# A spectral mixer with a feed-forward layer: the last inverse DFT in three matmuls of 128 rows for four pairs, in place of four of 96

## The chip, the cores and the metric

The kernel runs on one core of a Trainium2 chip. The metric is the device time of one execution in microseconds, the median of several runs; less is better. The matmul engine TensorE (PE in the profile; PEld is its loading of the stationary operand), VectorE (DVE), ScalarE (ACT) and GpSimd (POOL) run their own instruction streams in order; SyncE (SP) issues the DMAs, also in order.

## The reference

The input `x` is 8 × 3008 × 256. Along the 3008 time steps a real DFT is taken, the spectrum goes through a complex linear layer with a bias and a soft threshold, and comes back by the inverse DFT; the result goes through a feed-forward layer.

```python
X = np.fft.rfft(x, axis=1)
Yr = Xr @ w_r - Xi @ w_i + b_r
Yi = Xr @ w_i + Xi @ w_r + b_i
Yr = np.sign(Yr) * np.maximum(np.abs(Yr) - 0.01, 0)      # Yi likewise
y = np.fft.irfft(Yr + 1j * Yi, n=3008, axis=1)
h = y @ w_in                                              # 256 -> 2048
out = (h - np.tanh(h)) @ w_out                            # 2048 -> 256
```

## The kernel before

**The DFT in two steps.** 3008 = 64 × 47. The first step (`Forward`, and `Stacked` for batches 3 to 7) is a DFT over 47 and gives 24 frequencies; the second (`Spectrum.transform`, line 332) one over 64, 128 columns a matmul, the table read from another start for each frequency. After the linear layer `inverse` (lines 410 to 412) undoes the step over 64 and `put` writes the result `zo` to DRAM as `z`: 32 pairs of 96 rows (2 parities × real and imaginary × 24 frequencies) by 256 features.

**The last step**, which the change touches, is `Unit`: for a pair, 96 rows of `z` go to 94 time steps (2 × 47). A `Unit` takes up to four pairs. Its `load` (lines 484 to 495) brings the table (96 × 94 for each pair, into a piece of the tile `shared`) and `z` (tile `zin`); the features are the stationary operand in two halves of 128 columns, the table is the moving one. So for each pair and each half there is a matmul with 96 rows and 94 columns (line 504), in plain fp32, which the profile records as two MATMULs each. `both(k)` (line 522) does two pairs for both halves into one PSUM bank, 2 × 188 columns, and ScalarE copies these 376 columns into `raw`, or into `spill` for columns that belong to the next chunk (line 556). In the first stage `time(t)` does one half of all pairs of a unit.

**Chunks.** The feed-forward layer works on the 8 · 3008 columns in 47 chunks of 512 (`Chunk`). 94 does not divide 512, so the units of a chunk are cut so that a pair belongs to the chunk in which it begins: 4 pairs and then 1 or 2, and fewer at the end of a batch. The columns that stick out go to `spill`, at most 92 of them, and GpSimd copies them back (`unspill`, line 568) when `raw` is free. `sums` and `operands` make the operands of the feed-forward layer from `raw` on GpSimd and ScalarE. From chunk 3 on, this layer saves one matmul in eight in its first product (`Pair`, line 671); line 600 is the second product. Both stand on TensorE with 256 and 512 columns.

**The order of the work.** All engines and the DMA queue are recorded in an order written by hand. The feed-forward layer runs as a row of slots, 16 to a chunk, of some 3 us each; `plan` puts every other step into a slot with a rank: loads 0, the first transform's split 0.5 and its matmuls 7, `Spectrum.dft` 6, `inverse` 2.5, `Unit` 8, `sums` 9. In `run` (line 764) an inverse moves behind the `dft` of its slot if the slot has no step of rank 3, 4, 7 or 8. `unit_slots` looks for slots for the units in a window before the chunk is wanted, slots with a `dft` alone first and then the calmest; a unit's load is put five slots ahead of its first matmul, but not before the last `z` of its batch is written (`done_at`). Two `zin` buffers and two pieces of `shared` take turns. Within a slot, the steps share two PSUM buffers for all that is not the feed-forward layer.

Two places are tight, where a batch's first chunk is due soon after its last spectrum: chunk 5 (batch 1 begins in it; its unit has slot 74 and its load slot 72, the last `inverse` slot 71) and chunk 11 (batch 2; last `inverse` in slot 164, load in slot 165, matmuls in slot 168). In slots 71 to 86 the first transform of batch 2 runs, whose loads of x (eight, tile `xt`, two buffers, line 215) are put five slots ahead of their first matmul.

Of the kernel before, what the change touches and what calls it, by code (L numbers as in the profile page):

```python
# [18 lines left out]
LAM = 0.01  # L19

# [12 lines left out]
def dft_constants():  # L33
# [30 lines left out]
    i2 = i2.reshape(96, NP * 94)  # L64
# [4 lines left out]
def spectral_ffn(ctx, tc, x, w_r, w_i, b_r, b_i, w_in, w_out, x_twice, f1, f1s, f2, i1, i2, out):  # L69
    nc = tc.nc  # L70
    P = 128
# [179 lines left out]
    class Stacked:  # L251
# [3 lines left out]
        def load(self):  # L255
            if self.p == 0:
                a_dram[self.b] = dram.tile([2, NP, 96, D], F32, name=f"a_{self.b}", tag="a")
            if self.p % 6 == 4:
                self.xt = shared_piece("x2", 2 * 4 * 94 + 4 * D, 4 * D, 1).rearrange("p (a d) -> p a d", a=2)
# [45 lines left out]
    class Spectrum:  # L305
# [6 lines left out]
        def load(self):  # L312
# [4 lines left out]
            if self.b > 2:  # L317
                self.al = shared_piece("al", 2 * 4 * 94, 2 * D, 2)
                nc.sync.dma_start(out=self.al, in_=rows(a_dram[self.b][1], self.jp))
# [161 lines left out]
    class Unit:  # L481
        def __init__(self, b, p, n, home=None):
            self.b, self.p, self.n, self.home = b, p, n, home

        def load(self):
            if self.home is None:
# [4 lines left out]
                nc.sync.dma_start(out=self.table, in_=i2[:, self.p * 94:(self.p + self.n) * 94])  # L491
            else:
                self.zt = piece(self.home, [96, 4, D], F32, "zin")
                self.table = i2t[:, self.p * 94:(self.p + self.n) * 94]
            nc.sync.dma_start(out=self.zt[:, :self.n, :], in_=z_dram[self.b][self.p:self.p + self.n].rearrange("a p d -> p a d"))

        def time(self, t):
            ps = bank("ps_i2")
            self.multiply(ps, t)
            self.take(ps, t)  # L500

        def multiply(self, ps, t, at=0, which=None):
            for j, k in enumerate(which or range(self.n)):
                nc.tensor.matmul(  # L504
                    ps[:, at + j * 94:at + (j + 1) * 94], self.zt[:, k, t * P:(t + 1) * P],
                    self.table[:, k * 94:(k + 1) * 94], start=True, stop=True,
                )

        def pieces(self, k=0, n=None):
            first = self.b * S + (self.p + k) * 94  # L510
            lo, hi = first, first + (n or self.n) * 94
            while lo < hi:
                c = next(c for c in range(NCH) if begin[c] <= lo < begin[c] + sizes[c])
                end = min(hi, begin[c] + sizes[c])
                yield chunks[c], lo - begin[c], slice(lo - first, end - first)
                lo = end

        def take(self, ps, t):
            for chunk, at, cols in self.pieces():
                chunk.take(t, at, ps[:, cols])  # L520

        def both(self, k):
            ps = bank("ps_i2")
            m = min(2, self.n - k)
            n = m * 94
            for t in range(2):
                self.multiply(ps, t, t * n, range(k, k + m))
            pv = ps[:, :2 * n].rearrange("p (t n) -> p t n", t=2)
            for chunk, at, cols in self.pieces(k, m):
                chunk.take_both(at, pv[:, :, cols])  # L530
# [3 lines left out]
    class Chunk:  # L534
# [12 lines left out]
        def take(self, t, at, src):  # L547
# [4 lines left out]
            else:  # L552
                nc.scalar.copy(out=self.home(at, n)[:, t], in_=src)

        def take_both(self, at, src):
            nc.scalar.copy(out=self.home(at, src.shape[2]), in_=src)

        def home(self, at, n):
            if at > 0 or n >= 94:
                return raw[:, :, at:at + n]  # L560
            if self.spill is None:
                self.spill = work.tile([P, 2, 96], F32, name="spill", tag="spill")
                self.spilled = n
            return self.spill[:, :, :n]
# [284 lines left out]
    def plan():  # L849
# [22 lines left out]
        for b in range(2, B):  # L872
# [17 lines left out]
        for c in range(FIRST + 1, NCH):  # L890
            lo, hi = (-(-CT * k // 94) for k in (c, c + 1))
            units = []
            while lo < hi:
                n = min(4, hi - lo, NP - lo % NP)
                units.append(Unit(lo // NP, lo % NP, n))
                lo += n
            late = [u for u in units if c == first_chunk[u.b]]
            early = [u for u in units if c != first_chunk[u.b]]
            for some_units, window in ((early, (-14, -9 if late else -6)), (late, (-10, -6))):
                at = unit_slots(c, sum((u.n + 1) // 2 for u in some_units), window, max([done_at.get(u.b, 0) + 2 for u in some_units], default=0))  # L900
                for u in some_units:
                    mine = [at.pop(0) for _ in range(0, u.n, 2)]
# [57 lines left out]
    with tc.manual_schedule(engines={E.PE, E.Activation, E.DVE, E.Pool, E.SP}):  # L960
# [39 lines left out]
        i2t = work.tile([96, NP * 94], F32, name="i2", tag="i2", bufs=1)  # L1000
# [49 lines left out]
        for i in range(NU + 1):  # L1050
# [29 lines left out]
            if i in (5, 8):  # L1080
                sl = slice(0, 10 * 94) if i == 5 else slice(10 * 94, None)
# [10 lines left out]
        early_units = [Unit(0, 4 * k, 4, k) for k in range(5)] + [Unit(0, 20, 2, 5)]  # L1092
# [172 lines left out]
```

## Time and profile before

| | |
|---|---|
| median of 3 runs | 2609.38 us (2609.1 to 2612.08) |
| profiled execution | 2607.96 us |
| its span, first to last instruction | 2606.2 us |
| mean granted TensorE clock | 0.996 |
| from HBM, to HBM | 136.56 MB, 90.70 MB |
| loads of `z` for the last step | 93, of which 46 of 384 KB |

A row of a group reads: line, engine, operation, output<-inputs, shapes and count, then after the bar the busy time in us and the mean ns of one, then the idle time of the engine ahead of it and what ended it. A row of the timeline reads: start and length in us, engine, line, operation, and in brackets the idle time ahead of it with what ended that. Rows of SPq are DMA issues; in the list of DMA issues the last number is the median us from issue to landing. A row of the waits reads: who waited, for whom, us in total, times, longest.

### The profile page before, as it was taken

The page shows a single profiled execution, that of the slowest core. Times are in us where ns is not written, and L with a number is a line of the kernel's source. Part 1 is how long each engine was busy: PE and PEld are TensorE (multiplying, and loading weights), DVE is VectorE, ACT ScalarE, POOL GpSimd, SP SyncE. Part 2 cuts the span into 40 slices and gives each one's busy share as a digit, 9 for nine tenths or more (in the row PEclk, how much of TensorE's full clock was granted, in tenths as well). Part 3 has the DMA queues.
Part 4 walks back from the last instruction along what each step waited for, and adds up shares of the span by engine and source line. Part 5 has one row for each costly group of instructions (what it writes and reads, how often), then busy time and mean ns, then how long its engine had stood idle before and what let it go on. Part 6 is the DMA issues. An engine that isn't in the chain of part 4 may idle for free.

```text
span 2606.2 us, 43502 instructions
## 1 busy us (share of the span) xinstructions
PE 2578.3 (99%) x16297; PEld 2298.5 (88%) x16297; DVE 1833.1 (70%) x2742; ACT 1609.4 (62%) x2915; POOL 780.2 (30%) x885
## 2 busy tenths in 40 slices
PE   8999999999999999999999999999999999999999
PEld 6787797999899999899999999899998999999998
DVE  6786884777767777777776777777777666665655
ACT  5556566666666666666666666666666555565655
POOL 0003434333324432343323333243333223221210
PEclk8999999999999999999999999999999999999999
DMA  6521224322333333233323343232333122111000
GB/s 194 157 83 55 83 74 134 96 88 87 96 111 108 98 110 90 87 111 103 118 71 105 99 123 93 86 106 87 123 92 87 60 66 66 43 42 34 19 27 17
DMA packets 147315, 230.10 MB, mean 88 GB/s; under 512 B 15520, under 2 KB 87008, under 8 KB 147008
## 3 DMA queue, kind: packets, MB, share of 16 engines
q1 hardware_dynamic: 147104, 227.32, 28.8%
q8 instruction: 129, 2.11, 0.3%
q14 instruction: 82, 0.67, 0.1%
HBM read 136.56 MB, written 90.70 MB: 87 GB/s over the span
## 4 chain that ended last, share of the span: by engine, by line
PE 94%; DVE 2%; ACT 1%; issue 1%; POOL 1%; DMA 1%; SPq 0%; POOLq 0%; ACTq 0%; DVEq 0%
PE o L600 38%; PE H L671 33%; PE ps_v L359 4%; PE ps_i L504 4%; PE ps_f L332 3%; PE ps_t L359 2%; PE he L576 2%; PE ps_f L278 1%; PE ps_v L445 1%; PE ps_i L410 1%; PE ps_i L412 1%; PE ps_i L411 1%; PE oe L600 1%; DMA a<-st 0%; PE ps_i L468 0%
## 5 line engine op out<-in xcount | busy, mean ns | idle before, releaser
L671 PEld LDWEIGHTS H<-y_t,sum 128*128 128x128 f32 x3168 | 517.6, 188 | 103.8 <-DVE th L705 4.6
L709 ACT CAST gh<-th 128x1024 fp32r<-128x1024 f32 x352 | 370.7, 1053 | 350.7 <-DVE th L705 224.5
L600 PE MATMUL o<-gh,wout_l 128*128 128x512 f32 x1408 | 563.7, 400 | 0.0
L600 PE MATMUL o<-gl,wout_h 128*128 128x512 f32 x1408 | 554.7, 394 | 0.5 <-DVE gl L713 0.5
L600 PE MATMUL o<-gh,wout_h 128*128 128x512 f32 x1408 | 552.4, 392 | 0.0
L671 PE MATMUL H<-y_t,sum 128*128 128x256 f32 x3168 | 549.1, 282 | 1.4 <-ACT ot L611 0.6
L713 DVE TENSOR_TENSOR gl<-th,gh 128x1024 fp32r<-128x1024 f32 x352 | 439.5, 1249 | 66.6 <-ACT gh L709 64.4
L705 DVE TENSOR_TENSOR th<-H,th 128x1024 f32<-128x1024 f32 x352 | 428.7, 1218 | 4.7 <-ACT th L702 2.1
L702 ACT ACTIVATE th<-H 128x1024 f32<-128x1024 f32 x352 | 362.5, 1030 | 56.2 <-PE H L671 51.4
L687 DVE TENSOR_TENSOR H<-H,late 128x256 f32<-128x256 f32 x352 | 152.3, 433 | 318.6 <-PE H L671 278.7
L600 PEld LDWEIGHTS o<-gl,wout_h 128*128 128x128 f32 x1408 | 264.3, 188 | 61.8 <-DVE gl L713 1.5
L693 DVE TENSOR_TENSOR H<-H,late 128x256 f32<-128x256 f32 x352 | 151.7, 431 | 200.5 <-PE H L671 190.9
L671 PE MATMUL H<-y_b,win_h 128*128 128x256 f32 x1408 | 279.4, 280 | 0.0
L600 PEld LDWEIGHTS o<-gh,wout_l 128*128 128x128 f32 x1408 | 266.4, 189 | 7.4 <-ACT gh L709 0.5
L600 PEld LDWEIGHTS o<-gh,wout_h 128*128 128x128 f32 x1408 | 264.8, 188 | 7.6
L671 PE MATMUL H<-y_more,win_h 128*128 128x256 f32 x1408 | 262.9, 279 | 0.0
L679 ACT COPY late<-H 128x256 f32<-128x256 f32 x352 | 131.2, 373 | 197.1 <-PE H L671 194.1
L90 POOL TENSOR_TENSOR z_l<-mn,z_h 128x512 fp32r<-128x512 f32 x84 | 112.6, 1340 | 421.4 <-ACT z_h L89 257.9
L671 PEld LDWEIGHTS H<-y_more,win_h 128*128 128x128 f32 x1408 | 215.2, 188 | 5.9
L671 PEld LDWEIGHTS H<-y_b,win_h 128*128 128x128 f32 x1408 | 214.7, 188 | 0.1
L400 DVE TENSOR_TENSOR y<-tb,ps_v 64x256 f32<-64x256 f32 x384 | 160.7, 419 | 58.1 <-PE ps_v L359 45.2
L671 PE MATMUL H<-y_more,win_l 128*128 128x256 f32 x704 | 200.3, 285 | 0.0
(192 smaller groups left out, 4391.2 us busy)
## 6 DMA issues: line engine op xcount, KB each, us to landing
a<-st SPq DMA_DIRECT2D x188, 192.0 KB, 3.0
x<-in_x_twice SPq DMA_DIRECT2D x55, 512.0 KB, 4.8
at<-a SPq DMA_DIRECT2D x96, 256.0 KB, 3.4
z<-zo SPq DMA_DIRECT2D x96, 256.0 KB, 2.1
out<-ot SPq DMA_DIRECT2D x47, 512.0 KB, 3.1
zin<-z SPq DMA_DIRECT2D x46, 384.0 KB, 4.4
shared<-a SPq DMA_DIRECT2D x60, 256.0 KB, 3.7
shared<-in_x_twice SPq DMA_DIRECT2D x25, 512.0 KB, 5.0
```

Source lines behind the costliest of these rows:

```text
L90: rest.tensor_tensor(out=lo, in0=src, in1=hi.bitcast(F32), op=ALU.subtract)
L359: nc.tensor.matmul(dst, lhs[:, t], rhs[:, t, :], start=n == 0, stop=n == 5)
L400: nc.vector.tensor_tensor(out=y[ri * 64:(ri + 1) * 64, jj, :], in0=common(jj, ri), in1=self.vv[jj * 64:(jj + 1) * 64, ri * D:(ri + 1) * D] ...
L600: nc.tensor.matmul(self.o[t][:, :n], lhs[:, f, t * P:(t + 1) * P], rhs, start=f == 0 and k == 0, stop=f == NF - 1 and k == 2,)
L671: nc.tensor.matmul(dst, a, b, start=start and k == 0, stop=k == 2, skip_group_check=True)
L679: nc.scalar.copy(out=self.p7, in_=self.c11)
L687: nc.vector.tensor_tensor(out=self.c21, in0=self.acc, in1=self.p7, op=ALU.add)
L693: nc.vector.tensor_tensor(out=self.c22, in0=self.acc, in1=self.p7, op=ALU.add)
L702: nc.scalar.activation(out=self.th, in_=self.hp[:, :, :n], func=AF.Tanh)
L705: nc.vector.tensor_tensor(out=self.th, in0=self.hp[:, :, :self.n], in1=self.th, op=ALU.subtract)
L709: nc.scalar.copy(out=self.gh, in_=self.th)
L713: nc.vector.tensor_tensor(out=self.gl, in0=self.th, in1=h(self.gh), op=ALU.subtract)
```

## The change

A group is now always four whole pairs: 376 time steps and 384 rows of `z`, taken as three stationaries of 128 rows in place of four of 96. The table becomes block-wise: 384 rows by 376 columns with the four 96 × 94 blocks on the diagonal, of which each slice of 128 rows meets only some columns: the first 0 to 141 (pairs 0 and 1), the second 94 to 282 (1 and 2), the third 235 to 376 (2 and 3). The three matmuls have 141, 188 and 141 columns, overlap in PSUM and add up there. A group's table has 470 columns and 128 rows in place of 376 and 96.

```diff
+I2_COLUMNS = ((0, 141), (94, 282), (235, 376))
+I2_WIDTH = 470
...
-    i2 = i2.reshape(96, NP * 94)
+    i2 = i2.transpose(3, 0, 1, 2, 4, 5).reshape(NP // 4, 4, 96, 94)
+    i2, blocks = np.zeros((NP // 4, 384, 376)), i2
+    for k in range(4):
+        i2[:, 96 * k:96 * k + 96, 94 * k:94 * k + 94] = blocks[:, k]
+    i2 = np.concatenate([i2[:, 128 * k:128 * k + 128, lo:hi] for k, (lo, hi) in enumerate(I2_COLUMNS)], 2)
...
     class Unit:
...
-                self.zt = work.tile([96, 4, D], F32, name="zin", tag=tag, bufs=1)
-                self.table = shared_piece("i2", 0, 4 * 94, 2)[:96, :self.n * 94]
+                self.zt = work.tile([P, 3, D], F32, name="zin", tag=tag, bufs=1)
+                self.table = shared_piece("i2", 0, I2_WIDTH, 2)
...
-        def both(self, k):
-            ps = bank("ps_i2")
-            m = min(2, self.n - k)
-            n = m * 94
-            for t in range(2):
-                self.multiply(ps, t, t * n, range(k, k + m))
...
         def time(self, t):
             ps = bank("ps_i2")
+            at = 0
+            for k, (lo, hi) in enumerate(I2_COLUMNS):
                 nc.tensor.matmul(
+                    ps[:, lo:hi], self.zt[:, k, t * P:(t + 1) * P], self.table[:, at:at + hi - lo],
+                    start=k == 0, stop=k == 2, skip_group_check=True,
                 )
+                at += hi - lo
...
-                self.spill = work.tile([P, 2, 96], F32, name="spill", tag="spill")
+                self.spill = work.tile([P, 2, 368], F32, name="spill", tag="spill", bufs=1)
...
-                put(at[2 * ch] - 5, 0, f.load)
+                put(at[2 * ch] - 3, 0, f.load)
...
+            units = [Unit(g // 8, g % 8) for g in range(-(-CT * c // 376), -(-CT * (c + 1) // 376))]
...
-                        put(slot, 8, u.both, 2 * k)
+                        put(slot, 8, u.time, k)
...
         if c == first_chunk[1] and window[1] == -6:
-            return [zs - 4]
+            return [zs - 4, zs - 4]
...
-        early_units = [Unit(0, 4 * k, 4, k) for k in range(5)] + [Unit(0, 20, 2, 5)]
+        early_units = [Unit(0, k, k) for k in range(6)]
```

`both` is gone: a slot now does one half of the features of a whole group (`time`), again 376 columns of PSUM, and every group has two slots. A group belongs to the chunk in which it begins, so a chunk has one or two groups (two or four slots; before mostly three). Up to 368 columns go to `spill`, which has one buffer in place of two. All of the first six groups of batch 0 are done in the first stage (before: 22 pairs). At chunk 5 both halves stand in slot 74; at chunk 11 the halves stand in slots 166 and 168, the load still in 165. The loads of x for batch 2 come two slots later than before.

**TensorE in slots 165 and 166**, ahead of chunk 11. Names: `o` and `H` are the feed-forward layer, `ps_i` is the bank of the last step. Before, behind the half unit of slot 165:

```order
L504 MATMUL ps_i_7108<-shared,zin 128x94 x4
L600 MATMUL o_6981<-gh,wout_l 128x512
L600 MATMUL o_6981<-gh,wout_h 128x512
L600 MATMUL o_6981<-gl,wout_h 128x512
L671 MATMUL H_2183<-y_t_2125,sum_1_1929 128x256
L671 MATMUL H_2183<-y_t_2125,sum_0_1928 128x256 x2
```

Now, the same stretch:

```order
L511 MATMUL ps_i_7063<-shared,zin 128x141
L511 MATMUL ps_i_7063<-shared,zin 128x188
L511 MATMUL ps_i_7063<-shared,zin 128x141
L584 MATMUL o_6936<-gh,wout_l 128x512
L584 MATMUL o_6936<-gh,wout_h 128x512
L584 MATMUL o_6936<-gl,wout_h 128x512
L655 MATMUL H_2175<-y_t_2117,sum_1_1921 128x256
L655 MATMUL H_2175<-y_t_2117,sum_0_1920 128x256 x2
```

Four matmuls of 94 columns became three; behind them stand 15 matmuls of the feed-forward layer (the first six are shown) and then the three of the next group, batch 2's first, which before stood in slot 168, as four.

**TensorE in slot 55**, in batch 1's spectra. Before:

```order
L600 MATMUL o_2389<-gl,wout_h 128x512
L410 MATMUL ps_i_2734<-z_2_h,i_l 128x512
L411 MATMUL ps_i_2734<-z_2_h,i_h 128x512
L412 MATMUL ps_i_2734<-z_2_l,i_h 128x512
L332 MATMUL ps_f_2741<-f_125,at 128x2x64 x4
L504 MATMUL ps_i_2751<-shared,zin 128x94 x4
L600 MATMUL o_2421<-gh,wout_l 128x512
```

Now:

```order
L584 MATMUL o_2381<-gl,wout_h 128x512
L339 MATMUL ps_f_2724<-f_125,at 128x2x64 x4
L417 MATMUL ps_i_2734<-z_2_h,i_l 128x512
L418 MATMUL ps_i_2734<-z_2_h,i_h 128x512
L419 MATMUL ps_i_2734<-z_2_l,i_h 128x512
L584 MATMUL o_2413<-gh,wout_l 128x512
```

The unit has left this slot, so the spectrum's transform moved ahead of the inverse.

**SyncE ahead of the load for chunk 5.** Names: `z<-zo` are the writes of batch 1's spectra, `xt` the loads of x, `shared<-in_i` the table, `zin` the load of the group. Before:

```order
L215 DMA xt<-in_x 96x1024
L418 DMA z_2233<-zo 128x512
L215 DMA xt<-in_x 96x1024
L418 DMA z_2233<-zo 128x512
L215 DMA xt<-in_x 96x1024
L418 DMA z_2233<-zo 128x512 x2
L215 DMA xt<-in_x 96x1024
L491 DMA shared<-in_i 96x94
L495 DMA zin<-z_2233 96x256
L245 DMA a_3343<-st 96x4x256
```

Now:

```order
L222 DMA xt<-in_x 96x1024
L425 DMA z_2225<-zo 128x512
L222 DMA xt<-in_x 96x1024
L425 DMA z_2225<-zo 128x512 x2
L222 DMA xt<-in_x 96x1024
L500 DMA shared<-in_i 128x470
L505 DMA zin<-z_2225 128x3x256
L252 DMA a_3430<-st 96x4x256
L222 DMA xt<-in_x 96x1024
```

Three x loads instead of four stand ahead of the group's load, and the fourth has moved behind it and behind a write of `a`. The table is 240 KB here instead of 35.2, the load of `z` 384 KB instead of 96.

More of the change, by code (lines that the diff above doesn't have):

```diff
@@ L481, in spectral_ffn, with __init__ @@
     class Unit:
-        def __init__(self, b, p, n, home=None):
-            self.b, self.p, self.n, self.home = b, p, n, home
+        def __init__(self, b, g, home=None):
+            self.b, self.g, self.home = b, g, home
+            self.first = b * S + 376 * g
         def load(self):
+            table = slice(self.g * I2_WIDTH, (self.g + 1) * I2_WIDTH)
             if self.home is None:
@@ L497, in time @@
+                self.table = shared_piece("i2", 0, I2_WIDTH, 2)
+                nc.sync.dma_start(out=self.table, in_=i2[:, table])
+            else:
+                self.zt = piece(self.home, [P, 3, D], F32, "zin")
+                self.table = i2t[:, table]
+            src = z_dram[self.b][4 * self.g:4 * self.g + 4].rearrange("a p d -> (a p) d")
+            nc.sync.dma_start(out=self.zt, in_=src.rearrange("(k r) d -> r k d", r=P))
         def time(self, t):
             ps = bank("ps_i2")
-            self.multiply(ps, t)
@@ L500, in time @@
-            self.take(ps, t)
-        def multiply(self, ps, t, at=0, which=None):
-            for j, k in enumerate(which or range(self.n)):
+            at = 0
+            for k, (lo, hi) in enumerate(I2_COLUMNS):
                 nc.tensor.matmul(
-                    ps[:, at + j * 94:at + (j + 1) * 94], self.zt[:, k, t * P:(t + 1) * P],
-                    self.table[:, k * 94:(k + 1) * 94], start=True, stop=True,
-                )
[L509 to L516, printed above, removed]
@@ L532, in spectral_ffn @@
+                    start=k == 0, stop=k == 2, skip_group_check=True,
+                )
+                at += hi - lo
+            lo, end = self.first, self.first + 376
+            owner = max(lo // CT, FIRST)
+            while lo < end:
+                c = lo // CT
+                hi = min(end, CT * (c + 1))
+                chunks[c].take(t, lo - CT * c, ps[:, lo - self.first:hi - self.first], c > owner)
+                lo = hi
     Unit.turn = 0
@@ L545, in open, with take @@
                 )
-        def take(self, t, at, src):
+        def take(self, t, at, src, ahead):
             n = src.shape[1]
@@ L551, in take @@
                 nc.vector.tensor_tensor(out=self.yl[:, t, at:at + n], in0=src, in1=h(self.yh[:, t, at:at + n]), op=ALU.subtract)
[L552 to L561, printed above, removed]
-                self.spill = work.tile([P, 2, 96], F32, name="spill", tag="spill")
+                return
+            if ahead and self.spill is None:
+                self.spill = work.tile([P, 2, 368], F32, name="spill", tag="spill", bufs=1)
                 self.spilled = n
-            return self.spill[:, :, :n]
+            nc.scalar.copy(out=(self.spill if ahead else raw)[:, t, at:at + n], in_=src)
         def unspill(self):
@@ L899, in plan @@
             for some_units, window in ((early, (-14, -9 if late else -6)), (late, (-10, -6))):
-                at = unit_slots(c, sum((u.n + 1) // 2 for u in some_units), window, max([done_at.get(u.b, 0) + 2 for u in some_units], default=0))
+                at = unit_slots(c, 2 * len(some_units), window, max([done_at.get(u.b, 0) + 2 for u in some_units], default=0))
                 for u in some_units:
-                    mine = [at.pop(0) for _ in range(0, u.n, 2)]
+                    mine = [at.pop(0) for _ in range(2)]
                     last_two.append(mine[-1])
@@ L999, in spectral_ffn @@
         units = [WholeSpectrum(0, jp) for jp in range(NJ // 2)]
-        i2t = work.tile([96, NP * 94], F32, name="i2", tag="i2", bufs=1)
+        i2t = work.tile([P, NP * 94], F32, name="i2", tag="i2", bufs=1)
         lin = []
```

23 lines of the change are left out of this document (4 added, 19 removed).

## The prediction

> **What bounds the kernel now.** I read the page's busy times and its chain first, then busy time by stage, then the waits of the matmul engine, and last the order of time at the places that the change touches.
>
> ```profile
> PE 2578.3 (99%) x16297; PEld 2298.5 (88%) x16297; DVE 1833.1 (70%) x2742; ACT 1609.4 (62%) x2915; POOL 780.2 (30%) x885
> ...
> PE 94%; DVE 2%; ACT 1%; issue 1%; POOL 1%; DMA 1%; SPq 0%; POOLq 0%; ACTq 0%; DVEq 0%
> ```
>
> TensorE is busy 99% of the span and holds 94% of the chain that ended last. A share is an average, so the stages come next: start and end of the stretch, its length, then busy time (with instructions) of PE, PEld, DVE, ACT and POOL, the granted clock, DMA share and GB/s.
>
> ```profile
> 107.00:131.00 24.00, 22.10 (x126) 19.17 (x125) 15.61 (x33) 11.47 (x29) 0.00 (x0) 0.86 0.50 138
> ...
> 420.00:2450.00 2030.00, 2029.31 (x13316) 1839.84 (x13315) 1433.92 (x2081) 1282.45 (x2317) 665.08 (x755) 1.00 0.30 90
> ```
>
> From 420 to 2450 us the engine is busy 2029.3 of 2030 us at a granted clock of 1.00. The list of its waits from 420 to 2597 us has one row:
>
> ```profile
> PE ps_f L278 <- ACT late L679: 0.3, 1, 0.3
> ```
>
> So in that stretch a microsecond less of matmul work is a microsecond less of time, and what hangs on the other engines is hidden as long as no new wait appears. Before 420 us that is not given.
>
> **The matmuls.** The change replaces 512 matmuls of 94 columns (two per pair, 256 pairs) by 384: for each of 64 groups and two halves of the features a set of 141, 188 and 141 columns. An fp32 matmul is recorded twice, hence 936 + 88 records:
>
> ```profile
> L504 PE MATMUL ps_i<-shared,zin 96*128 96x94 f32 x936 | 122.2, 271 | 1.4 <-DMA zin<-z 1.4
> L504 PE MATMUL ps_i<-i,zin 96*128 96x94 f32 x88 | 12.2, 299 | 1.9 <-DVE st L242 1.4 <-DMA zin<-z 0.5
> ```
>
> The mean of 271 ns is the length of a record and not the distance to the next one, since records overlap. The price is read from the starts around four such matmuls (eight records) that stand between matmuls of 512 columns:
>
> ```profile
> 720.57 0.39 PE L600 MATMUL o<-gh,wout_h 128*128 128x512 f32 x1
> 720.79 0.39 PE L600 MATMUL o<-gl,wout_h 128*128 128x512 f32 x1
> 721.02 1.03 PE L504 MATMUL ps_i<-shared,zin 96*128 96x94 f32 x8
> 721.83 0.48 PE L600 MATMUL o<-gh,wout_l 128*128 128x512 f32 x1
> 722.15 0.39 PE L600 MATMUL o<-gh,wout_h 128*128 128x512 f32 x1
> 722.38 0.39 PE L600 MATMUL o<-gl,wout_h 128*128 128x512 f32 x1
> ```
>
> From 720.79 to 722.15 are 1.36 us. Without the four, two steps of 512 columns would lie there, 0.23 us each (722.38 − 722.15). Four matmuls of 94 columns thus take 0.90 us, 0.225 each. Four of 128 columns with 128 rows, elsewhere:
>
> ```profile
> 787.71 0.39 PE L600 MATMUL o<-gl,wout_h 128*128 128x512 f32 x1
> 787.94 1.05 PE L332 MATMUL ps_f<-f,at 128*128 128x128 f32 x8
> 788.75 0.48 PE L600 MATMUL o<-gh,wout_l 128*128 128x512 f32 x1
> 789.07 0.39 PE L600 MATMUL o<-gh,wout_h 128*128 128x512 f32 x1
> ```
>
> Again 1.36 − 0.46 = 0.90. So 94 and 128 columns cost the same, and 96 and 128 rows too: up to 128 columns there is a floor, and 34 columns in each matmul are paid for without use. Above it the fp32 matmuls of the first stage give the price (two of 256 columns, then one of 512, then the next):
>
> ```profile
> 64.57 1.03 PE L445 MATMUL ps_t<-wr_f,sf 128*128 128x256 f32 x4
> ...
> 65.43 1.02 PE L468 MATMUL ps_i<-mn,i_f 128*128 128x512 f32 x2
> ...
> 66.29 0.50 PE L332 MATMUL ps_f<-f,at 128*128 128x128 f32 x3
> ```
>
> 0.86 / 2 = 0.43 us for 256 columns, 0.86 for 512: 1.68 ns a column. By that 141 columns cost 0.237 and 188 cost 0.316, a set 0.79, and 0.11 is saved. By a straight line from 0.225 at 128 to 0.43 at 256 (1.60 ns a column) they cost 0.246 and 0.321, a set 0.81, and 0.09 is saved. I take 0.10: 128 × 0.10 = **12.8 us**. The starts are given to 0.01, so the ends are 0.08 and 0.12: 10.2 to 15.4.
>
> The Trainium skill, "TensorE: Matmul & The Clock Gate", section Back-to-back issue gap, gives N / 2.4 + 2.5 ns for a matmul's step on a warm array, and "FP8 and Floating Point Precision", section TensorE Precision Notes, four passes for true fp32. By these pages, as an estimate, 128 columns take 223 ns, which the row of 0.225 bears out, 256 take 437, where the row has 430, and a set takes 813 ns: that would save 11.1 us in place of 12.8, and the forecast would stand 1.7 us higher. The rows at 256 and 512 columns lie below the pages' price, so I stay with the rows.
>
> **Where it is not all gained.** Twelve of the 128 sets run before 131 us, where the clock is 0.86 and PE is busy 22.1 of 24 us, because it waits for PSUM buffers and for ScalarE and VectorE. I count half of their 1.2 us as lost there: +0.6 (0 to 1.2).
>
> **First group of batch 1 (slot 74).** Before, its matmuls wait for their load:
>
> ```profile
> 402.31 1.30 POOL L90 TENSOR_TENSOR x_l<-xt,x_h 94x512 fp32r<-94x512 f32 x1 [0.62 <-ACT x_h L89]
> ...
> 403.63 0.33 SPq L215 DMA_DIRECT2D xt<-in_x  x1
> ...
> 404.60 0.31 SPq L495 DMA_DIRECT2D zin<-z  x1
> ...
> 405.94 0.40 PE L230 MATMUL ps_f<-x_l,f_h 94*96 94x512 f32 x1
> 407.74 0.66 PE L504 MATMUL ps_i<-shared,zin 96*128 96x94 f32 x4 [1.41 <-DMA zin<-z]
> ```
>
> SyncE's queue stands at the x load until GpSimd frees that buffer at 403.61; the load of z behind it is issued at 404.60 and the matmuls start 1.4 us late. With the x loads two slots later, one x load fewer lies ahead, and the table and z come as soon as z is written. The last two writes of z:
>
> ```profile
> 396.86 0.85 SPq L418 DMA_DIRECT2D z<-zo  x2
> ...
> z<-zo SPq DMA_DIRECT2D x2, 256.0 KB, 4.3
> ...
> zin<-z SPq DMA_DIRECT2D x46, 384.0 KB, 4.4
> DMA to landing us min/median/max: 1.9/4.1/7.5
> ```
>
> Issued by 397.7 and landed 4.3 us later at 401.6 (the second write starts at about 397.3), the load of 384 KB (before: 96) lands 4.4 us on, at 406.0; the matmuls are due at 405.94 + 0.23 = 406.17. The load is just hidden. The x load that was passed loses nothing: it cannot start before 403.61 in either place. But both halves now stand in this slot, three PSUM buffers are wanted of two, and the second half must wait for the evacuation of the transform ahead of it:
>
> ```profile
> 406.86 0.58 ACT L242 COPY st<-ps_f 96x512 f32<-96x512 f32 x1
> ```
>
> It ends at 407.44, the first set at 406.17 + 0.79 = 406.96: a wait of 0.5. So 1.4 goes and 0.5 comes, near **−1.0**; with the slowest landing of all loads of z, 7.5 us, the load would be there at 409.1, 2.9 us late. The ends are −1.4 and +2.9.
>
> **First group of batch 2 (slot 166).** Here a wait is added. The group's first half now stands one slot behind its load, where the load had three slots.
>
> ```profile
> 719.05 0.34 SPq L418 DMA_DIRECT2D z<-zo  x1
> ...
> 722.64 0.30 SPq L495 DMA_DIRECT2D zin<-z  x1
> ...
> 724.37 0.28 PE L671 MATMUL H<-y_more,win_l 128*128 128x256 f32 x1
> ...
> zin<-z SPq DMA_DIRECT2D x1, 192.0 KB, 2.5
> ```
>
> The load is issued when z has landed, at 722.64; the new place on PE is ahead of the row at 724.37. Two pairs (192 KB) landed in 2.5 us at this place, 384 KB take 4.4 as a median and 7.5 at most: 725.1, 727.0 or 730.1, so a wait of 0.8, 2.7 or 5.8 us. Behind it on PE stand the FFN's matmuls, and everyone waits for those. The size speaks for the second, the place for the first; I take a value between them: **+2.0**.
>
> **Slot 55.** The set that stood there is gone, and by the rule in line 764 the inverse moves behind the transform. Before, the transform waits there:
>
> ```profile
> PE ps_f L332 <- ACT zo L417: 0.7, 1, 0.7
> ```
>
> I take **−0.7** (to 0, if the next step then waits).
>
> **What is hidden.** ScalarE copies the same columns in 27 instructions more, on an engine that is busy 62%. GpSimd's copies out of the spill grow to up to 2×368 columns:
>
> ```profile
> L568 POOL COPY raw<-spill 128x40 f32<-128x40 f32 (+42 forms) x43 | 12.6, 292 | 0.6
> 644.35 0.27 POOL L568 COPY raw<-spill 128x100 f32<-128x100 f32 x1
> 653.23 0.47 ACT L556 COPY raw<-ps_i 128x376 f32<-128x376 f32 x1
> ```
>
> With one spill buffer instead of two, ScalarE must wait for that copy; it is over 8 us before ScalarE writes next, at the closest pair of slots that the new plan has (143 and 145). A copy four to seven times as long costs nothing there. Were the cover gone, each microsecond of it would be one on ScalarE's queue ahead of the tanh. Tables load 240 KB a group for 144, on engines of which 30% are in use.
>
> **The sum.** −12.8 + 0.6 − 1.0 + 2.0 − 0.7 = −11.9. The profiled execution took 2607.96 us (span 2606.2), 1.4 below the median of 2609.38. Against that median: **2597.5 us**.
>
> **The rivals.** *Late loads, no change.* If both loads land at the slowest row's 7.5 us, slot 74 costs +2.9 and slot 166 +5.8; with 0.09 a set (11.5) and nothing kept of the early sets (+1.2) and slot 55, −1.6 is left: 2607.8. For it speaks that the loads are four and two times as big as before at these places; against it that 7.5 is the slowest of all, and 4.1 the median. It decides when the two waits pass 7 us together.
>
> *Odd columns, slower.* 141 is odd, and the second table starts at word 141, the third output at column 235. If such a matmul read or wrote at half rate, a set would take 2 × 0.474 + 0.316 = 1.26 us, 0.36 more than before: 128 × 0.36 = 46 us slower, with the other terms 2656. It decides from 0.05 us above my price per odd matmul. For it: no matmul in the profile has an odd width. Against it: the spectrum's matmuls (line 332) read runs of 32 columns from odd starts too and cost 0.225.
>
> *Columns for nothing, much faster.* If the added columns ran beside the next weight load, a set would cost 3 × 0.225 = 0.68: −28.8, in all 2581.5. Against it: 256 columns cost 0.43. The Trainium skill's same section states such a flat price for sustained streams (81 ns at 128 columns, 131 at 512); this trace has 0.23 us at 512 and does not bear it out.
>
> That the change doesn't do what it says is excluded: the order shows three matmuls in each set.
>
> **How the numbers follow.** Forecast 0.84, late loads 0.10, odd columns 0.04, free columns 0.02. About 0.2% (5.2 us) can be told from no change here. Faster: 0.84 + 0.02 = 0.86; same 0.10; slower 0.04. The range takes the ends of the work and of the waits. Below: −15.4 + 0.6 − 1.4 + 0.8 − 0.7 = −16.1, 2593.3. Above: −10.2 + 0.6 − 1.0 + 5.8 − 0.7 = −5.5, 2603.9.
>
> **Right or wrong.** In the changed profile the sets between matmuls of 512 columns should show 0.79 to 0.81 us; the waits from 420 to 2597 us one new row, z's load at about 724 us, of 1 to 3 us, and else nothing; at 406 us no wait for the load but one of about 0.5 for a PSUM buffer; at 304 us none for zo. Sets above 0.85 us, or a list of waits that grows throughout, would make the prediction wrong.

## The result and the profile after

The changed kernel takes 2592.56 us (median of 6 runs, 2591.33 to 2593.88) against 2610.56 us (6 runs, 2608.62 to 2612.37): a ratio of 0.9931, 95% interval 0.9918 to 0.9944. The forecast was 2597.5 us, its range 2593.3 to 2603.9. The direction and most of the mechanism hold, but the gain is 18 us where 12 were forecast, and the time lies 0.7 us below the range. The profiled execution took 2592.27 us, its span is 2590.5 us, 15.7 less than before's.

The page's busy times of the changed kernel, and below them its busy time by stage (columns as in the prediction):

```profile
PE 2562.1 (99%) x16041; PEld 2283.3 (88%) x16041; DVE 1835.7 (71%) x2742; ACT 1608.5 (62%) x2942; POOL 795.3 (31%) x885
```

```profile
107.00:131.00 24.00, 20.79 (x117) 17.81 (x117) 16.66 (x35) 11.97 (x32) 0.00 (x0) 1.00 0.46 141
420.00:2450.00 2030.00, 2029.43 (x13175) 1838.84 (x13173) 1443.38 (x2092) 1288.47 (x2354) 679.11 (x757) 1.00 0.30 92
```

TensorE is busy 16.2 us less (2578.3 − 2562.1), ScalarE and VectorE about as long as before. From 420 to 2450 us PE still never stops. From 107 to 131 us the clock is now 1.00 where it was 0.86.

The list of PE's waits from 420 to 2580 us has one row, the same as before; the wait for z's load that the prediction put at 724 us is not there:

```profile
PE ps_f L285 <- ACT late L663: 0.3, 1, 0.3
```

The sets, in order of time (start, duration):

```profile
716.62 0.39 PE L584 MATMUL o<-gh,wout_h 128*128 128x512 f32 x1
716.84 0.39 PE L584 MATMUL o<-gl,wout_h 128*128 128x512 f32 x1
717.08 0.96 PE L511 MATMUL ps_i<-shared,zin 128*128 128x141 f32 x6
717.78 0.49 PE L584 MATMUL o<-gh,wout_l 128*128 128x512 f32 x1
718.11 0.39 PE L584 MATMUL o<-gh,wout_h 128*128 128x512 f32 x1
718.34 0.40 PE L584 MATMUL o<-gl,wout_h 128*128 128x512 f32 x1
```

Read as in the prediction: 718.11 − 716.84 = 1.27, less two steps of 0.23, is 0.81 us a set, against 0.90 for four matmuls of 94 columns. Odd widths cost nothing extra, and the added columns are not free.

**Where the 15.7 us lie.** The feed-forward layer's matmuls stand in the same order in both kernels, so the start of the n-th of them can be compared. Taken are the matmuls into `H` of the product that saves one in eight (line 671 before, 655 after). The 1st, the 451st and the 7201st start here, before:

```profile
264.56 0.62 PE L671 MATMUL H<-y_t,sum 128*128 128x256 f32 x3 [0.63 <-ACT ot L611]
...
451.02 0.28 PE L671 MATMUL H<-y_b,win_l 128*128 128x256 f32 x1
...
2546.48 0.28 PE L671 MATMUL H<-y_b,win_l 128*128 128x256 f32 x1
```

and here after:

```profile
262.43 0.63 PE L655 MATMUL H<-y_t,sum 128*128 128x256 f32 x3 [0.62 <-ACT ot L595]
...
448.50 0.28 PE L655 MATMUL H<-y_b,win_l 128*128 128x256 f32 x1
...
2531.04 0.28 PE L655 MATMUL H<-y_b,win_l 128*128 128x256 f32 x1
```

The changed kernel leads by 2.1 us, then by 2.5, then by 15.4. Between the last two there are 110 sets, hardly a wait and full clock: 12.9 us. At 0.09 a set that is 9.9; another 0.45 is two matmuls that before has more in this stretch (442 of 94 columns, where 110 sets of four are 440). Some 2.5 us are left in which neither the trace's waits nor its clock show anything: the feed-forward matmuls themselves follow each other faster. After 2200 us matmuls of 256 columns start 118.3 to 119.1 ns apart before and 117.6 to 117.9 after (means of 100 us).

### The profile page after: what moved, and what is told of

Read it like the earlier page. It is cut to its first block, busy times and chain, and to the rows that moved or that the text cites. A ratio compares the mean times of both kernels' runs of the same rounds, so it can differ in the third digit from the quotient of the medians.

```text
span 2590.5 us, 42898 instructions
## 1 busy us (share of the span) xinstructions
PE 2562.1 (99%) x16041; PEld 2283.3 (88%) x16041; DVE 1835.7 (71%) x2742; ACT 1608.5 (62%) x2942; POOL 795.3 (31%) x885
## 4 chain that ended last, share of the span: by engine, by line
PE 94%; DVE 2%; ACT 1%; issue 1%; POOL 1%; DMA 1%; POOLq 0%; DVEq 0%; ACTq 0%; SPq 0%
PE o L584 38%; PE H L655 33%; PE ps_v L366 4%; PE ps_i L511 4%; PE ps_f L339 3%; PE ps_t L366 2%; PE he L560 2%; PE ps_f L285 1%; PE ps_v L452 1%; PE ps_i L417 1%; PE ps_i L419 1%; PE ps_i L418 1%; PE oe L584 1%; DMA a<-st 0%; PE ps_i L475 0%
```

## Experiments

I had two theories for the surplus. A: it is the difference between two executions. B: it belongs to the change.

**Both kernels again.**

> The changed kernel again, unchanged. Its first profile has a set of three at 0.80 us (0.09 less than four before, 11.4 us over 128 sets), and 4.4 us of gain beside the sets: 2.0 before 264 us, where before had a stretch at half clock at 113 to 121 us that the changed kernel had not (it had one at 393 to 397), and 2.6 after 2000 us, where matmuls of 256 columns follow each other every 117.7 ns instead of 118.6. Theory A (these are differences between two executions): the stretch at half clock lies elsewhere or is gone, and the distance late in the program is not again below before's by 0.8 ns; the median lies 11 to 15 us under before. Theory B (they belong to the change): no stretch at 113 us, the distance is again about 117.7 ns, the median lies 16 to 20 us under before.

> The kernel before again, unchanged: median within 1.5 us of the other runs of before. Theory A: the stretch at half clock at 113 to 121 us is not there again, or the distance of matmuls of 256 columns after 2000 us is nearer to 118. Theory B: both are there again.

Measured: 2592.04 us (5 runs, 2589.38 to 2594.54; ratio 0.9931, interval 0.9919 to 0.9944) for the changed kernel, 2609.08 for the kernel before (11 runs, 2606.95 to 2612.07; ratio 0.9998, interval 0.9989 to 1.0007). From the 451st to the 7201st matmul the two profiles of before differ by 0.25 us, the two of the changed kernel by 0.42, and the mean distances between matmuls of 256 columns repeat to 0.2 ns in most stretches of 100 us. So that part is no chance: A falls, B stands. The stretch at half clock came as B had it too: at 113 us again before, and not in the changed kernel. The rest of this study asks what in the change does it.

**The loads of x alone, and the rest without them.** In the changed kernel:

```diff
-                put(at[2 * ch] - 3, 0, f.load)
+                put(at[2 * ch] - 5, 0, f.load)
```

and the reverse in the kernel before.

> The changed kernel with the loads of x of batch 2 where they were before (five slots ahead), so the matmuls alone. If these loads matter at chunk 5 as the prediction put it: the wait for the load of z at about 405 us is back, 1.5 to 4 us now that the load is four times as big, and the median lies that much above the changed kernel. If they do not matter: no wait over 0.5 us there, and the median within 1 us of the changed kernel.

> The kernel before with only the loads of x two slots later, four matmuls of 94 columns as before. By the prediction's step for chunk 5: the wait of 1.4 us for the load of z at 406 us goes, 0.9 to 1.6 us are gained, no more. If the later loads are what the prediction missed: 4 to 8 us are gained.

Measured: 2596.8 us (interval of the ratio to before 0.9935 to 0.996), 4.2 to 4.8 above the changed kernel; and 2607.6 us (0.998 to 0.9998), 1.5 to 2.8 below before. The wait, first in the changed kernel and then with the loads back in their place:

```profile
404.21 0.39 PE L237 MATMUL ps_f<-x_l,f_h 94*96 94x512 f32 x1
404.44 0.96 PE L511 MATMUL ps_i<-shared,zin 128*128 128x141 f32 x6
405.77 1.07 PE L511 MATMUL ps_i<-shared,zin 128*128 128x141 f32 x6 [0.36 <-ACT st L249]
```

```profile
405.48 2.37 PE L511 MATMUL ps_i<-shared,zin 128*128 128x141 f32 x12 [3.36 <-DMA zin<-z]
```

With the loads two slots later z is there in time, and the second half waits 0.36 us for the evacuation of the transform ahead of it, as forecast. Without them the load, four times as big as before, is 3.36 us late, and right behind that wait the clock falls to half from 406.6 to 409.8 us, which by an estimate costs half of these 3.2 us more. So the loads' new slots are not worth the 1.0 us by which the wait at this place shrank, but 3 and more: they pay for what whole groups would have cost here. In the kernel before, the later loads take away the wait of 1.41 us (none stands in that profile); the medians fall by 1.5 to 2.8 us, not by 4 to 8. The missing microseconds are not theirs.

**Four matmuls again, everywhere and in the first stage.** Everything but the sets as changed:

```diff
-            for k, (lo, hi) in enumerate(I2_COLUMNS):
+            for k in range(4):
                 nc.tensor.matmul(
-                    ps[:, lo:hi], self.zt[:, k, t * P:(t + 1) * P], self.table[:, at:at + hi - lo],
-                    start=k == 0, stop=k == 2, skip_group_check=True,
+                    ps[:, 94 * k:94 * k + 94], self.zt[:96, k % 3, t * P:(t + 1) * P], self.table[:96, 94 * k:94 * k + 94],
+                    start=True, stop=True,
                 )
```

In the second kernel the four stand only where `self.home is not None`, which are the 12 sets of the first stage.

> The changed kernel with each set done by four matmuls of 96 rows and 94 columns again (on the same tiles, so the numbers that it gives are not the inverse transform); loads, slots, spill and memory stay as changed. If the sets by themselves are worth the 0.09 us each of the trace: 11.4 us above the changed kernel (2592.3), about 2603.7. If the stretch at half clock at 113 us in the kernel before also hangs on the sets: 13 to 15 us above. If the gain lies mostly in the plan: less than 8.

> The changed kernel with four matmuls of 96 rows and 94 columns in the 12 sets of the first stage alone (the first six groups' output is not the inverse transform). Sets alone: 12 x 0.09 = 1.1 us slower, clock at full speed at 113 us. If four matmuls in these sets bring the stretch at half clock: it is back at 113 us, and 2 to 4 us are lost.

Measured: 2605.62 us for four everywhere (10 runs; ratio to before 0.9987, interval 0.9978 to 0.9997), 13.1 to 13.6 above the changed kernel. From the 451st to the 7201st matmul it is 10.7 us for 110 sets. One microsecond of that is a wait at batch 2's first group, which the changed kernel does not have:

```profile
725.12 1.10 PE L510 MATMUL ps_i<-shared,zin 96*128 96x94 f32 x8 [0.99 <-ACT H L662]
```

The row names a copy on ScalarE, but the set does not need it (in the changed kernel it starts at 720.34, and that copy at 720.94); the last part of the load of z landed at 725.03. The other 9.7 us are 0.088 a set. So the gain hangs on the sets and not on the plan of whole groups. Of the 2.7 us that are left of it without them more is said below. In the first stage alone: 2593.64 us (4 runs, 2593.18 to 2595.6), 1.1 to 1.6 above the changed kernel, which is about the sets' own 1.1 and not the 2 to 4 that a stretch at half clock was expected to cost. It is there again all the same:

```profile
107.00:131.00 24.00, 22.11 (x129) 19.39 (x129) 15.45 (x33) 11.23 (x27) 0.00 (x0) 0.86 0.44 142
```

Over all profiles of this study a stretch at half clock that begins between 109 and 116 us stands in 9 of the 10 profiles that run these sets as four matmuls, and in 3 of the 10 that run them as three. The Trainium skill, "TensorE: Matmul & The Clock Gate", section Part 1: The HAM clock gate, says that the clock is set by how busy the array has been, in windows of about 3.4 us that run on freely, and that the same kernel therefore shows more or fewer slow matmuls from run to run. The profiles agree: of the two of the changed kernel one has a stretch at half clock at 393 us and the other has none there. What the stretch at 113 us costs can't be told from this pair, whose medians differ by no more than the sets do. All 20 profiles together say a little: the 12 that have it come to the 1st matmul into `H` at 264.8 us on average, the 8 others at 262.1.

**Is the load at chunk 11 just in time?** The prediction had put +2.0 us there.

```diff
-put(max(mine[0] - 5, 48, done_at.get(u.b, 0) + 1, last_two[-3] + 1), 0, u.load)
+put(max(mine[0] - 5, 48, done_at.get(u.b, 0) + (2 if u.b == 2 else 1), last_two[-3] + 1), 0, u.load)
```

> The changed kernel with the load of batch 2's first group one slot later, behind a load of x of 512 KB. If the cover at this place is as thin as the prediction had it, the matmuls at 720 us wait 2 to 6 us for z and the median rises by as much. If the load has time to spare there (no wait shows at 720 us in the changed kernel): under 1 us.

Measured: 2594.41 us (4 runs, 2592.89 to 2595.73), 1.9 to 2.4 above the changed kernel, with intervals to before that overlap. The profile decides: one new wait, of 1.04 us.

```profile
719.58 0.39 PE L655 MATMUL H<-y_b,win_h 128*128 128x256 f32 x2
721.01 1.04 PE L511 MATMUL ps_i<-shared,zin 128*128 128x141 f32 x6 [1.04 <-DMA zin<-z]
```

So there is no time to spare, but it was enough. SyncE's queue at this place, changed kernel, and what it waited for:

```profile
715.09 0.34 SPq L425 DMA_DIRECT2D z<-zo  x1
715.52 0.38 SPq L500 DMA_DIRECT2D shared<-in_i  x1
717.19 0.37 SPq L505 DMA_DIRECT2D zin<-z  x1
```

```profile
SPq L505 <- DMA z<-zo: 1.2, 1, 1.2
```

and before:

```profile
719.48 1.56 SPq L491 DMA_DIRECT2D shared<-in_i  x1
```

```profile
SPq L495 <- DMA z<-zo: 1.5, 1, 1.5
SPq L491 <- PE H L671: 1.1, 1, 1.1
```

From the write of z to the issue of its load passed 3.6 us before (719.05 to 722.64) and 2.1 now (715.09 to 717.19). The table's load stood 1.1 us before, for PE by the list, but it is not what held the load behind it: that one waited on for z. Before, 15 of the 16 parts of z's write had landed by 721.06, 2.0 us behind its issue, and the last at 722.62; now all 16 by 717.13, again 2.0 us behind. How late the last part comes varies: over the nine profiles with sets of four at this place 2.3 to 3.6 us pass from write to load, over the ten with sets of three and the load in its slot 2.1 to 2.3. Why is not shown. The load's last part lands at 720.13, 2.9 us behind its issue, and the matmuls follow at 720.34 and don't wait: 0.2 us to spare. With four matmuls everywhere z's write is late again (issue of the load at 722.01, 3.4 us behind the write), the load takes 3.0 us, and the wait of 0.99 us shown above is the one that had been forecast here. I had taken the old issue time and the median landing of 4.4 us: the first was one execution's, and the other too long for this place.

**The memory.** What else does the change alter for matmuls that it doesn't touch? Its spill buffer is 2944 bytes wide in place of twice 768, and the feed-forward layer's buffers `gl`, `gh` and `th` are allocated behind it: in the built program they start 1408 bytes higher. `gl` and `gh` are the moving operands of the second layer. In the kernel before I changed nothing but the width of its two spill buffers:

```diff
-                self.spill = work.tile([P, 2, 96], F32, name="spill", tag="spill")
+                self.spill = work.tile([P, 2, 184], F32, name="spill", tag="spill")
```

> The kernel before with its two spill buffers 184 columns wide instead of 96, nothing else: together as large as the one of 368, so that what lies behind them in SBUF moves to where the change puts it. After 2200 us the distance of matmuls of 256 columns is 118.3 to 119.1 ns in three profiles of before and 117.6 to 117.9 in three of the changed kernel. If the addresses set it: 117.6 to 117.9 here, and about 2 to 3 us less than before. If not: 118.3 to 119.1, and before's time.

Measured: 2603.67 us (10 runs, 2603.13 to 2605.68) against 2608.33: ratio 0.9983, interval 0.9973 to 0.9992. From the 451st to the 7201st matmul 2.7 us are gained, steadily, and the distance after 2200 us is 117.8 to 118.6 ns. Against this kernel, whose buffers stand where the change puts them, the changed kernel gains 10.2 us in that stretch: the 0.45 of the two matmuls more, 0.089 for each of 110 sets, and nothing is left over. (The changed kernel's own profile is the fastest of the five with its sets and buffers; against their mean 0.085 a set is left, here and with four matmuls everywhere.)

I then moved the buffers to other places: in the kernel before by widths of 112, 140, 104 and 100 columns; in the changed kernel by a width of 372, and by taking the spill buffer from the pool of `gl`, `gh` and `th`, where it comes to stand behind all three:

```diff
-                self.spill = work.tile([P, 2, 368], F32, name="spill", tag="spill", bufs=1)
+                self.spill = ffn.tile([P, 2, 368], F32, name="spill", tag="spill", bufs=1)
```

With one more such line right behind the first tile that uses the place of `gh`, or of `gl`, it stands between `gh` and `th`, or between `gl` and `gh`.

> The changed kernel with the spill buffer behind the feed-forward layer's buffers th, gh and gl instead of ahead of them: these stand 2944 bytes lower than in the changed kernel, 1536 lower than before. Nothing else changes. If their addresses set the distance of matmuls that follow each other (theory A): the lead over the changed kernel changes steadily from 264 to 2530 us, by at least 0.5 us in one direction or the other, as it did between before and the one with buffers of 184 columns (2.7 us); which direction, the theory does not say. If the addresses do not matter (theory B): within 0.3 us over that stretch, as between two runs of one kernel.

> The kernel before with spill buffers of 112 columns: th, gh and gl 256 bytes higher. Theory A: a steady change against before between 264 and 2546 us, of -3 to +3 us. Theory B: within 0.3 us.

> The kernel before with spill buffers of 140 columns: th, gh and gl 704 bytes higher, half of what gave 2.7 us. Theory A: a steady change against before between 264 and 2546 us, of -3 to +3 us, and not the same as at 256 and at 1408 bytes. Theory B: within 0.3 us.

> The changed kernel with the spill buffer between gh and th: gl and gh 2944 bytes lower, th where the change has it. Behind all three it lost 4 us against the changed kernel between 264 and 2531 us. If the addresses of gl and gh count, which TensorE reads: 3 to 5 us lost in that stretch again. If th counts, which only ScalarE and VectorE use: within 0.5 us of the changed kernel there.

> The changed kernel with the spill buffer between gl and gh: gl alone 2944 bytes lower, gh and th where the change has them. If each buffer counts by itself: a third to two thirds of the 4 us (1.3 to 2.7) lost between 264 and 2531 us. If gl does not count: within 0.5 us. If it is the place of gl, gh and th to each other: anything from -3 to +8.

> The kernel before with spill buffers of 104 columns: gl, gh and th 128 bytes higher, the remainder of their address by 256 is 192, as with 1408 bytes. If the remainder counts: 2.2 to 3.2 us gained against before between 450 and 2546 us. If the size of the shift counts, so that a small one does nothing, as 256 bytes did: within 0.4 us.

> The kernel before with spill buffers of 100 columns: gl, gh and th 64 bytes higher, remainder 128 by 256. If the remainder counts: a steady change of more than 0.5 us in one direction between 450 and 2546 us; the direction is not known. If the size of the shift counts: within 0.4 us.

> The changed kernel with the spill buffer 372 columns wide: gl, gh and th 32 bytes higher, remainder 224 by 256. If the remainder counts, and the slow one is near 0: up to 7 us lost between 450 and 2531 us, or up to 3 gained. If only steps of 64 bytes count, or a small shift does nothing: within 0.5 us.

Measured (start of `gl` in bytes in the built program, with its remainder by 256; time from the 451st to the 7201st matmul into `H`, for the altered kernels against the one each was made from; of this the part in steps from a matmul into `H` to the next start, and from a matmul of `gh` or `gl` to the next; median, and the interval of its ratio to before):

| kernel | `gl` starts at, remainder | stretch, us | behind `H` | behind `gh`, `gl` | median, us | interval |
|---|---|---|---|---|---|---|
| before | 203328, 64 | 2095.5 | 799.7 | 904.4 | 2608.1 to 2610.6 | |
| spill 112 | +256, 64 | −0.3 | −0.1 | −0.2 | 2609.23 | 0.9991 to 1.0009 |
| spill 104 | +128, 192 | −2.9 | −3.2 | −0.2 | 2606.08 | 0.9979 to 0.9997 |
| spill 184 | +1408, 192 | −2.7 | −3.1 | −0.1 | 2603.67 | 0.9973 to 0.9992 |
| spill 100 | +64, 128 | +4.8 | −3.0 | +7.8 | 2614.74 | 1.001 to 1.003 |
| spill 140 | +704, 0 | +7.1 | −2.8 | +9.9 | 2617.73 | 1.0021 to 1.0047 |
| changed | 204736, 192 | 2082.5 | 797.1 | 904.0 | 2592.56 | 0.9918 to 0.9944 |
| spill 372 | +32, 224 | +11.4 | +2.4 | +9.4 | 2606.68 | 0.9982 to 1.0 |
| spill behind all three | −2944, 64 | +4.0 | +3.1 | +1.4 | 2598.94 | 0.9947 to 0.9972 |
| spill between `gh` and `th` | −2944, 64; `th` stays | +3.8 | +2.9 | +1.4 | 2596.88 | 0.994 to 0.9973 |
| spill between `gl` and `gh` | −2944, 64; `gh`, `th` stay | +3.1 | +1.4 | +2.1 | 2594.72 | 0.993 to 0.9962 |

Profiles with the same sets and buffers agree to 0.5 us in the stretch and to 0.3 in the two parts, but for waits. The runs are from several chips, but kernels on one chip differ as much: widths 104 and 100 ran on one, 112 and 140 on another. The intervals of the last two rows overlap that of the changed kernel; for these two the profiles alone speak.

The same can be read from the busy times of 450 to 2450 us: the number of PE's matmuls that fit in, with the engine as busy and the clock as full. Before, 184 columns, 140 columns:

```profile
450.00:2450.00 2000.00, 1999.31 (x13136) 1813.79 (x13135) 1418.18 (x2062) 1260.27 (x2278) 652.59 (x743) 1.00 0.29 89
```

```profile
450.00:2450.00 2000.00, 1999.43 (x13148) 1814.31 (x13147) 1419.28 (x2066) 1259.84 (x2279) 653.07 (x743) 1.00 0.30 89
```

```profile
450.00:2450.00 2000.00, 1999.54 (x13094) 1807.33 (x13093) 1412.96 (x2057) 1256.61 (x2274) 653.41 (x743) 1.00 0.30 89
```

The changed kernel, and the same with its buffers 32 bytes higher:

```profile
450.00:2450.00 2000.00, 1999.43 (x12997) 1812.78 (x12995) 1427.61 (x2073) 1267.09 (x2317) 667.76 (x747) 1.00 0.29 91
```

```profile
450.00:2450.00 2000.00, 1999.71 (x12929) 1805.91 (x12928) 1420.56 (x2063) 1261.29 (x2306) 663.98 (x743) 1.00 0.30 91
```

The last row has 68 matmuls fewer, at 2000 / 12997 = 0.154 us 10.5 us of work. The list of PE's waits of this kernel from 450 to 2500 us is as short as the others:

```profile
PE ps_f L285 <- ACT late L663: 0.3, 1, 0.3
```

The two parts in the table show two different effects. At the remainders 0, 128 and 224 it is the steps of 512 columns that grow, those of `gl` and `gh` against the weights: in the kernel with 372 columns from 231 to 236 ns apart on average in stretches of 100 us to 235 to 240. But between 64 and 192, the 2.7 us that the change brought with it, these steps are the same to 0.2 us, and the 3 us lie in the steps of 256 columns, of matmuls that read neither `gl` nor `gh` and whose own operands stand where they stood.

What follows: it is the remainder by 256 and not the size of the shift (128 bytes do what 1408 do, 256 do nothing); it is the places of `gl` and `gh`, not of `th`, and that of `gl` alone makes 3.1 of the 4.0 us, a little more than I had allowed it; and the change had, without meaning it, put them at the best remainder of the five that I tried. The remainder does not say everything: 64 against 192 is 2.7 us in the kernel before and 4.0 in the changed one. By which access the places act is not shown either. TensorE reads `gl` and `gh`, but ScalarE writes `gh` and VectorE `gl` while other matmuls run, and no run separates the reading from the writing. 32 bytes higher, most of the change's gain would have been gone.

**Other operands.** The `y` tiles, moving operands of the first layer, have the remainder 160 in both kernels, the weights 128. One kernel lifts the y tiles, and all between, to 192 by allocating a bias ahead of them; the other lifts the weights `win` and `wout` to 192 too:

```diff
         below = const.tile([P, 1], F32, name="below")
+        rebias = const.tile([P, 1], F32, name="rebias")
...
-        rebias = work.tile([P, 1], F32, name="rebias", bufs=1)
```

```diff
+    below = const.tile([P, 1], F32, name="below")
+    rebias = const.tile([P, 1], F32, name="rebias")
     win_h = const.tile([P, 2, FF], F32R, name="win_h")
...
-        below = const.tile([P, 1], F32, name="below")
...
-        rebias = work.tile([P, 1], F32, name="rebias", bufs=1)
```

> The changed kernel with one bias of 4 bytes allocated ahead of the y tiles instead of behind: they and all that lies between stand 32 bytes higher, at remainder 192 by 256 instead of 160; gl, gh and th keep theirs. If the rule holds for every moving operand: 2 to 10 us gained, mostly in the matmuls of 256 columns (118.3 ns apart, against a half of 234 for 512 columns, 117). If it is peculiar to gl and gh: within 0.5 us between 450 and 2531 us.

> As the one with the y tiles at 192, and the weights win and wout (stationary operands) at 192 instead of 128. If only moving operands count: within 0.5 us of that kernel between 450 and 2531 us. If reading the weights counts too: a steady change of more than 0.5 us.

Measured: 2590.69 us (5 runs, 2589.77 to 2592.84; interval 0.9918 to 0.9944), 0.8 us gained between the 451st and the 7201st matmul, more than two executions differ by and less than the rule had promised; and not where it had promised: the steps behind `H`, whose operands were moved, take 0.4 us more, those behind `gh` and `gl`, whose operands stayed, 2.3 less. By the median this kernel can't be told from the changed one. With the weights lifted as well, 2605.73 us (0.9979 to 0.9998), 12.9 us lost in the stretch against the changed kernel and 13.8 against the one with the y tiles alone, in both kinds of steps (7.0 and 6.1), though `gl` and `gh` stayed. The same window of it, 78 matmuls short of the changed kernel:

```profile
450.00:2450.00 2000.00, 1999.71 (x12919) 1813.65 (x12919) 1420.07 (x2063) 1260.91 (x2304) 665.27 (x743) 1.00 0.30 91
```

So 192 is not a good remainder by itself. Either the places of buffers to each other count, or the weights' own; no run here separates these.

## Why the prediction was right or wrong

- **The matmuls, −12.8 (10.2 to 15.4): right, a little high.** 0.085 to 0.089 a set from two pairs of kernels with their buffers in the same places, 10.9 to 11.4 us over 128 sets. The estimate from the Trainium skill ("TensorE: Matmul & The Clock Gate", section Back-to-back issue gap, times the four passes of "FP8 and Floating Point Precision", section TensorE Precision Notes) was 0.087, the two from the rows 0.09 and 0.11; the prediction took 0.10, and 0.09 would have been nearer.
- **The early stage, +0.6 (0 to 1.2): not resolved.** The forecast makes a lead of 0.6 us out of the 1.2 of twelve sets. The lead at the 1st matmul into `H` is 2.1 us in one pair of profiles and 0.0 in the other. The mean of the ten profiles with three matmuls there is 2.2 us ahead of that of the ten with four, but each ten scatter by some 1.8. The clock there, which the prediction took as given, went with the sets; and PE's list of waits from 107 to 131 us had 1.4 us for VectorE and 0.5 for the load of z, none for ScalarE.
- **Slot 74, −1.0: right**, 1.41 us became 0.36, with the forecast releaser. The load itself is not "just hidden": issued at 395.25 us and landed 3.7 us later, it had 5.5 us to spare, because the writes of z ahead of it landed in 2.2 us instead of 4.3 and stand earlier. (Its table is 235 KB by the list of issues, not 240.)
- **Slot 166, +2.0 (0.8 to 5.8): wrong.** No wait. The step that failed is "the load is issued when z has landed, at 722.64", 3.6 us behind z's write, and then 4.4 us to land: it was issued 2.1 us behind the write and landed 2.9 later, 0.2 ahead of the matmuls. The mechanism was right: in the kernel with four matmuls everywhere, where the issue came 3.4 us behind the write, 0.99 us of wait appeared, and with one load of x ahead of it 1.04.
- **Slot 55, −0.7: wrong**, the wait is still there:

```profile
303.75 1.16 PE L339 MATMUL ps_f<-f,at 128*128 128x128 f32 x8 [0.72 <-ACT zo L424]
```

I had put the row of the wait to the place where the order changes. Counted by the feed-forward layer's matmuls it belongs to an earlier slot, which still has inverse, transform and set in that order; the slot that the change reorders had no wait before:

```profile
317.00 0.40 PE L412 MATMUL ps_i<-z_l,i_h 128*128 128x512 f32 x1
317.23 1.05 PE L332 MATMUL ps_f<-f,at 128*128 128x128 f32 x8
```

- **What is hidden: the step that cost the range.** The copies out of the spill are hidden, as said. But the prediction looked at the spill buffer for its time alone, and not for what its size moves: 2.7 us, on matmuls that the change doesn't touch. No term and no rival stood for it, and it is more than the 0.7 us by which the range missed.

The sum with measured terms: −11.1 for the sets, −1.0 for slot 74, −2.7 for the memory, nothing for slots 166 and 55 and for the clock of the early stage, gives −14.8, against 15.7 between the two profiled executions. That the forecast of −11.9 came as near as it did is in part luck: the sets 1.7 too high and a gain of 0.7 at slot 55 that did not come stood against a loss of 2.0 that did not come and 2.7 that had no term. Between the medians the gain is 18.0, with 14.6 to 21.4 by the interval. The 3 us between may be in part the stretches at half clock in the first 410 us, which vary from one execution to the next; that is not shown.

## What to carry to other kernels

Ask of a change what its buffers push: where TensorE is the bound and never waits, the places of buffers in memory can be worth as much as the edit, here from −2.9 to +12.9 us. To price an edit, compare kernels with the same allocation (a buffer made wider than needed does it), and compare the starts of the same instructions, whose lead tells a wait, which is a step, from a changed rate, which is a slope. Take a wait out before dividing by the number of sets. Before costing a moved load at its old issue time, look at what held the queue there and at more than one execution, and match a wait to its place by counting instructions, not by the time alone.

## What was not expected of the hardware

Matmuls with nothing to wait for, at full clock, repeat their distance from one execution to the next, and change it with the places of buffers. With the weights at 128, the second product's matmuls of 512 columns were fast at remainders by 256 of 64 and 192 for `gl` and `gh` and about 1% slower at 0, 128 and 224 (8 to 10 us in 904). The first product's matmuls of 256 columns, which do not read these buffers, were 0.3 to 0.4% slower at 64 and 224 than at 192 (2.4 to 3.2 us in 800). With the weights at 192, both were slow at 192. And a stretch at half clock in the first stage went with how the same work was cut into matmuls: 9 profiles of 10 against 3 of 10.
